# A new prologue for a fused attention and mixer kernel: first loads by heads, finer turning of the first pairs, and pair 2's norms moved into the first slot

## The chip, the cores and the metric

The kernel runs on one core of one Trainium2 chip. The metric is the device time of one execution in microseconds (us). Each kernel is executed several times, and nearly all executions of one kernel agree within 0.3%. The kernel before strays more: 6 of its 41 executions in the rounds of these runs took 388.9 to 392.6 us, the others 386.1 to 387.7. An execution more than 1.5% above the fastest of its kernel is called slow and is left out of every ratio; the quoted medians are of all executions. One execution of each kernel is recorded by the hardware profiler. Its span, from the first to the last instruction, is about 1.8 us shorter than its device time.

## The reference

The program is cosine attention with 8 batches and 12 heads, followed by a token mixer and a channel mixer.

```
q_n = q / (norm(q) + 1e-6);  k_n = k / (norm(k) + 1e-6)      # (8, 12, 448, 64)
attn = softmax(q_n @ k_n^T / 0.1) @ v
x  = attn as (8, 448, 768)
u  = x + (relu(x^T @ w_tok1) @ w_tok2)^T                     # token mixer, 448 -> 256 -> 448
out = u + relu(u @ w_ch1) @ w_ch2                            # channel mixer, 768 -> 1536 -> 768
```

## The kernel before

Two heads make a "pair"; there are 48 pairs, six to a batch. The order of instructions is written by hand, and each engine takes its own instructions in that order. A pair passes through these steps: q and k are loaded; their squares are taken on ScalarE or GpSimd; VectorE sums them; ScalarE does Ln and Exp (the square root); VectorE does the reciprocal; GpSimd or VectorE scales; TensorE transposes ("turns") and VectorE copies; TensorE scores; ScalarE takes the exp in four parts. GpSimd also issues the loads of the token weights (w1t, w2n). A "slot" is the time in which one pair's four exps run. While pair i scores, later pairs are prepared.

```
def load_rows(i, nm, src, bufs):                 # k of pairs 0 to 2 on the scalar queue, all else on sync
    ...
    (nc.scalar if nm == "k" and i < 3 else nc.sync).dma_start(...)

def norms(i, a0=0, a1=2, dve=False):
    if dve:                                      # VectorE's part
        nc.vector.tensor_reduce(out=rn, in_=ne, axis=AXX.X, op=ALU.add)
        nc.vector.reciprocal(out=rn, in_=rn)
        return
    nc.scalar.activation(out=rn, in_=..., func=AF.Ln, bias=tiny[0:n])      # ScalarE's part
    nc.scalar.activation(out=ne[:, :, 0], in_=rn, func=AF.Exp, scale=0.5)

# the prologue, from pair 0's scores on
score(0, 0)
score(0, 1)
norms(1, dve=True)
scale(1, 0)                    # GpSimd: k of pair 1
scale(1, 1, nc.vector)         # VectorE: q of pair 1
sums(2)
norms(2)
cast_v(0)
score(0, 2)
warm(8)
tpose(1)                       # eight turnings
score(0, 3)
warm(6)
norms(2, dve=True)
square(3, 1, act=True)
square(3, 0)
...
for i in range(1, NPAIR):      # slots 1 to 5
    if i == 1:
        scale(2, 0)                    # GpSimd
        scale(2, 1, nc.vector)
    else:
        scaled(i + 1)                  # both on GpSimd
        ...
    load_qk(i + 6)
    score(i, 0)
    score(i, 1)
    sums(i + 2)
    norms(i + 2)
    ...
    pv_wide(i - 1)
    norms(i + 2, dve=True)
    cast_v(i)
    square(i + 3, 0)                   # GpSimd: k of pair i + 3
    ...
    score(i, 2)
    score(i, 3)
    tpose(i + 1)
    ...
    if i == 1:
        place_w2()                     # GpSimd: copy of the second token weight
    if 2 <= i < NPAIR - 1:
        udma(i - 2)                    # u of pair 0, 1, 2 of batch 0, turned by a DMA
```

## Time and profile before

| | before |
|---|---|
| time, median of 4 executions | 386.58 us (386.31 to 392.23; without the last, a slow one, 386.36) |
| span of the profiled execution | 385.4 us |
| length of a slot | 4.19 us |
| ScalarE / GpSimd busy in 15.38 to 40.76 us | 24.51 / 24.42 of 25.38 us |
| TensorE busy after 40.76 us | 339.25 of 344.64 us |

The program has three stages. First is a chain of single waits; then six slots in which ScalarE and GpSimd are both full; then TensorE is full to the end. A delay in the first two stages moves the third. The prediction shows the lines for these. Its median of 386.36 us came from the three executions known then, the slow one among them.

### The profile page before, as it was taken

The page shows a single profiled execution, that of the slowest core. Times are in us where ns is not written, and L with a number is a line of the kernel's source. Part 1 is how long each engine was busy: PE and PEld are TensorE (multiplying, and loading weights), DVE is VectorE, ACT ScalarE, POOL GpSimd, SP SyncE. Part 2 cuts the span into 40 slices and gives each one's busy share as a digit, 9 for nine tenths or more (in the row PEclk, how much of TensorE's full clock was granted, in tenths as well). Part 3 has the DMA queues.
Part 4 walks back from the last instruction along what each step waited for, and adds up shares of the span by engine and source line. Part 5 has one row for each costly group of instructions (what it writes and reads, how often), then busy time and mean ns, then how long its engine had stood idle before and what let it go on. Part 6 is the DMA issues. An engine that isn't in the chain of part 4 may idle for free.

```text
span 385.4 us, 10226 instructions
## 1 busy us (share of the span) xinstructions
PE 372.2 (97%) x4124; PEld 243.3 (63%) x4124; DVE 217.4 (56%) x520; ACT 226.6 (59%) x398; POOL 237.8 (62%) x383
## 2 busy tenths in 40 slices
PE   5989899999999999999999999999999999999995
PEld 4566566677656666667666666667666666665564
DVE  7789766777535674557545674566544674241032
ACT  5899687845665456855675466764675466601400
POOL 8799987979567667668557767768657733000000
PEclk9799999999999999999999999999999999999998
DMA  8999999995984888768894887977996745114023
GB/s 214 263 244 235 157 235 190 226 222 112 243 191 116 200 204 201 175 168 177 213 195 117 172 204 185 197 173 181 198 217 122 134 120 133 15 54 97 0 67 99
DMA packets 115423, 64.21 MB, mean 167 GB/s; under 512 B 71728, under 2 KB 111792, under 8 KB 115376
## 3 DMA queue, kind: packets, MB, share of 16 engines
q1 hardware_dynamic: 108944, 57.62, 68.2%
q0 software_dynamic: 5616, 5.21, 8.9%
q10 hardware_dynamic: 816, 0.73, 0.7%
q8 instruction: 32, 0.52, 0.6%
q14 instruction: 15, 0.12, 0.1%
HBM read 43.45 MB, written 11.01 MB: 141 GB/s over the span
## 4 chain that ended last, share of the span: by engine, by line
PE 87%; DMA 4%; ACT 4%; DVE 2%; POOL 1%; issue 1%; ACTq 0%; DVEq 0%; POOLq 0%
PE psF L449 28%; PE psG L433 28%; PE psO L362 9%; PE psS L323 7%; PE psU L407 5%; PE psR L393 5%; DMA ut<-u 3%; ACT pt L324 3%; PE psQ L330 2%; PE psO L345 1%; DMA qf<-in_q_dram 1%; PE pst L300 1%; ACT sq L235 1%; POOL sq L237 1%; DVE ssq L253 0%
## 5 line engine op out<-in xcount | busy, mean ns | idle before, releaser
L324 ACT ACTIVATE pt<-psS 128x896 f16<-128x896 f32 (+1 forms) x156 | 132.6, 916 | 58.2 <-PE psS L323 57.8
L433 PE MATMUL psG<-ut,wc1t 128*128 128x448 f16 x576 | 116.8, 352 | 0.5 <-DMA ut<-u 0.5
L449 PE MATMUL psF<-wc2t,gt 128*128 128x384 f16 (+2 forms) x684 | 116.2, 323 | 0.0
L436 ACT ACTIVATE gt<-psG 128x448 f16<-128x448 f32 x96 | 51.8, 540 | 63.0 <-PE psG L433 63.0
L276 POOL TENSOR_TENSOR kq<-kf,rn 128x384 f16<-128x384 f32 (+1 forms) x48 | 42.8, 892 | 73.6 <-DVE rn L262 70.3
L449 PEld LDWEIGHTS <-gt 128*128 128x128 f16 x684 | 64.2, 98 | 38.0
L433 PEld LDWEIGHTS <-wc1t 128*128 128x128 f16 x576 | 53.8, 98 | 44.9 <-issue 0.7
L453 DVE TENSOR_TENSOR ost<-psF,u 128x384 f32<-128x384 f32 (+2 forms) x65 | 34.5, 531 | 57.1 <-PE psF L449 56.9
L253 DVE TENSOR_REDUCE ssq<-sq 128x15 f32<-128x960 f32 (+2 forms) x49 | 55.8, 1140 | 4.2 <-ACT sq L235 3.6
L396 DVE TENSOR_SCALAR rt<-psR 128x256 f16<-128x256 f32 x48 | 20.1, 419 | 59.5 <-PE psR L393 59.4
L276 POOL TENSOR_TENSOR kq<-qf,rn 112x512 f16<-112x512 f32 x45 | 46.9, 1043 | 3.0
L323 PE MATMUL psS<-qk 64*128 64x448 f16 x312 | 41.7, 359 | 2.7 <-DVE qk L302 2.5
L237 POOL TENSOR_TENSOR sq<-kf 128x384 f32<-128x384 f32 (+1 forms) x46 | 40.1, 872 | 1.2 <-DMA kf<-in_k_dram 1.2
L362 PE MATMUL psO<-vt,pt 128*128 128x65 f16 (+1 forms) x1056 | 40.3, 193 | 0.2 <-DVE ut L424 0.2
L237 POOL TENSOR_TENSOR sq<-qf 112x512 f32<-112x512 f32 x39 | 40.5, 1039 | 0.0
L362 PEld LDWEIGHTS <-pt 128*128 128x128 f16 (+1 forms) x1056 | 35.2, 97 | 4.0 <-PE psS L323 1.0
L366 DVE TENSOR_TENSOR x<-psO,rec 128x256 f16<-128x256 f32 x84 | 35.6, 424 | 2.9
L410 DVE TENSOR_TENSOR u<-psU,x 128x512 f16<-128x512 f32 x48 | 32.3, 674 | 4.8 <-PE psU L407 3.6
L393 PEld LDWEIGHTS <-w1t 128*128 128x128 f16 x384 | 25.0, 98 | 9.0 <-issue 2.3
L407 PEld LDWEIGHTS <-w2t 128*128 128x128 f16 x384 | 24.9, 98 | 7.8 <-issue 1.5
L393 PE MATMUL psR<-x,w1t 128*128 128x128 f16 x384 | 29.3, 219 | 0.4 <-DVE u L410 0.3
L407 PE MATMUL psU<-rt,w2t 128*128 128x128 f16 x384 | 29.3, 219 | 0.2 <-DVE qk L302 0.2
(54 smaller groups left out, 282.8 us busy)
## 6 DMA issues: line engine op xcount, KB each, us to landing
qf<-in_q_dram SPq DMA_DIRECT2D x48, 224.0 KB, 4.2
kf<-in_k_dram SPq DMA_DIRECT2D x36, 192.0 KB, 3.4
vf<-in_v_dram SPq DMA_DIRECT2D x36, 192.0 KB, 3.7
vf<-in_v_dram SPq DMA_DIRECT2D x12, 224.0 KB, 7.3
out_dram<-ost SPq DMA_DIRECT2D x8, 336.0 KB, 3.6
wc1t<-in_moe_w_ch_dram POOLq DMA_DIRECT2D x4, 576.0 KB, 10.2
wc2t<-in_moe_w_ch_dram POOLq DMA_DIRECT2D x2, 1152.0 KB, 14.0
out_dram<-ost SPq DMA_DIRECT2D x8, 288.0 KB, 3.3
```

Of the source, the lines that this page charges most:

```text
L237: nc.gpsimd.tensor_mul(out=dst, in0=src, in1=src)
L253: nc.vector.tensor_reduce(out=st["ssq"][0:n, sl], in_=st["sq"][0:n, sl], axis=AXX.X, op=ALU.add)
L276: eng.tensor_tensor(out=kq[0:p, a, 0:n].rearrange("p c g e -> p g c e"), in0=st["kq"[a]][:].rearrange("p (g c) e -> p g c e", g=2), in1=_b ...
L323: nc.tensor.matmul(psS[:, hh, 0:S], qk[hb, c * n:c * n + 128], qm[hb], start=True, stop=True)
L324: nc.scalar.activation(out=pts[i % 2][0:n, 2 * S * c:2 * S * (c + 1)].rearrange("p (h s) -> p h s", h=2), in_=psS[0:n, :, 0:S], func=AF.Ex ...
L362: nc.tensor.matmul(psO[:, m, 0:E + 1], pts[i % 2][0:n, at:at + 128], vt[0:n, i % HP, nch * hh + c, 0:E + 1], start=(old(i) and c == 0), st ...
L366: nc.vector.tensor_tensor(out=st["x"][:, :, hh * E:(hh + 1) * E], in0=psO[:, :, 0:E], in1=_bcast_free(rec[:], E), op=ALU.mult)
L393: nc.tensor.matmul(psR[:, tt], w1t[:, w1[m], tt * 128:(tt + 1) * 128], st["x"][:, m], start=(m == 0), stop=(m == 3))
L407: nc.tensor.matmul(psU[:, m], w2t[:, tt, lo:lo + 128], st["rt"][:, tt], start=(tt == 0), stop=(tt == TT - 1))
L433: nc.tensor.matmul(psG[:, 0:S], wc1t[:, dt, ct * 128:(ct + 1) * 128], ut[b][:, dt].rearrange("p m s -> p (m s)")[:, lo:lo + S], start=(dt ...
L436: nc.scalar.activation(out=gt[:, ct, (b % 2) * S:(b % 2 + 1) * S], in_=psG[:, 0:S], func=AF.Relu)
L449: nc.tensor.matmul(psF[:, 0:hi - lo], gt[:, ct, at:at + 128], wc2t[:, ct, lo:hi], start=(ct == 0), stop=(ct == CT - 1))
```

## The change

The intent is to let the first exps start sooner. Pair 0's q and k are each loaded as two halves, one head on the sync queue and one on the scalar queue, and every other load goes on sync. Pair 0's k is scaled, turned and copied in halves. Pair 1's norms come before the first exp on ScalarE, and its q and k are turned one by one, so that only four turnings stand ahead of pair 0's last score. ScalarE's load of its function table is issued earlier, too. Pair 2's norms and scalings leave the prologue for slot 1, and its q is scaled by GpSimd, not by VectorE.

```
+    def load_first(a, src):
+        t = qkv.tile([SC, QS, E], FP32, name=f"{a}f_0", tag=f"{a}f", bufs=7)
+        for g, eng in ((0, nc.sync), (1, nc.scalar)):
+            eng.dma_start(out=t[:, NCH * g:NCH * (g + 1)].rearrange("p c e -> p (c e)"),
+                          in_=src[0, g].rearrange("(p c) e -> p (c e)", c=NCH))
+        return t
 ...
-            (nc.scalar if nm == "k" and i < 3 else nc.sync).dma_start(
+            nc.sync.dma_start(
 ...
-        scale(0, 0)
+        scale_part(0, 0, 0, 2, nc.gpsimd)
+        scale_part(0, 0, 2, NCH, nc.gpsimd)
 ...                                         # sums of pair 1 split, norms(1) before the first exp
         norms(1, dve=True)
+        scale(1, 1, nc.vector)
         scale(1, 0)
-        scale(1, 1, nc.vector)
-        sums(2)
-        norms(2)
         cast_v(0)
         score(0, 2)
-        warm(8)
-        tpose(1)
+        warm(4)
+        tpose(1, 1, 2)
+        warm(4)
+        tpose(1, 0, 1)
         score(0, 3)
         warm(6)
-        norms(2, dve=True)
+        sums(2)
 ...
         for i in range(1, NPAIR):
-            if i == 1:
-                scale(2, 0)
-                scale(2, 1, nc.vector)
-            else:
+            if i > 1:
                 scaled(i + 1)
 ...
             score(i, 0)
+            if i == 1:
+                norms(2)
+                norms(2, dve=True)
+                scaled(2)
             score(i, 1)
```

More of the change, by code (lines that the diff above doesn't have):

```diff
@@ L265, in norms, with scale_part @@
         nc.scalar.activation(out=ne[:, :, 0], in_=rn, func=AF.Exp, scale=0.5)
+    def scale_part(i, a, c0, c1, eng):
+        st = pipe[i]
+        if "kq16" not in st:
+            st["kq16"] = kqs[i % 4]
+        rn = st["rn"][0:SC, lay(i)[0][a]]
+        eng.tensor_tensor(out=st["kq16"][0:SC, a, c0:c1].rearrange("p c g e -> p g c e"),
+                          in0=st["kq"[a]][:].rearrange("p (g c) e -> p g c e", g=2)[:, :, c0:c1],
+                          in1=_bcast_free(rn.rearrange("p (g c) -> p g c", g=2)[:, :, c0:c1], E), op=ALU.mult)
     def scale(i, a, eng=None):
@@ L289, in scaled, with tpose @@
         scale(i, 1)
-    def tpose(i, a0=0, a1=2):
+    def tpose(i, a0=0, a1=2, c0=0, c1=NCH):
         st = pipe[i]
@@ L296, in tpose @@
             st["qk"] = qk[:, 0:2 * NCH * n].rearrange("p (a c s) -> p a c s", a=2, c=NCH)
-        pst = ps.tile([128, a1 - a0, NCH, n], FP16, name=f"pst_{i}_{a0}", tag="b")
+        pst = ps.tile([128, a1 - a0, c1 - c0, n], FP16, name=f"pst_{i}_{a0}_{c0}", tag="b")
         for a in range(a0, a1):
-            for c in range(NCH):
-                nc.tensor.transpose(pst[:, a - a0, c, :], st["kq16"][:n, a, c].rearrange("p g e -> p (g e)"),
+            for c in range(c0, c1):
+                nc.tensor.transpose(pst[:, a - a0, c - c0, :], st["kq16"][:n, a, c].rearrange("p g e -> p (g e)"),
                                     id16[:n, :n])
-        nc.vector.tensor_copy(out=st["qk"][:, a0:a1], in_=pst[:])
+        nc.vector.tensor_copy(out=st["qk"][:, a0:a1, c0:c1], in_=pst[:])
     def tpose_dma(i):
@@ L516 @@
     with tc.manual_schedule():
-        for i in range(3):
-            load_qk(i)
+        half[0] = {}
+        pipe[0] = {"q": load_first("q", q), "k": load_first("k", k)}
+        nc.scalar.add_instruction(mybir.InstLoadActFuncSet(
+            name=nc.get_next_instruction_name(), act_func_set_id=ACT_SET_LN_EXP,
+            ins=[], outs=[]))
+        load_qk(1)
+        load_qk(2)
         load_v(0)
@@ L525 @@
         load_v(3)
-        nc.scalar.add_instruction(mybir.InstLoadActFuncSet(
-            name=nc.get_next_instruction_name(), act_func_set_id=ACT_SET_LN_EXP,
-            ins=[], outs=[]))
         weights_tok1()
@@ L535 @@
         sums(0, 0, 1)
+        norms(0, 0, 1)
         norms(0, 1, 2, dve=True)
-        norms(0, 0, 1)
         scale(0, 1, nc.vector)
         norms(0, 0, 1, dve=True)
-        scale(0, 0)
+        scale_part(0, 0, 0, 2, nc.gpsimd)
+        scale_part(0, 0, 2, NCH, nc.gpsimd)
         square(1, 1, act=True)
@@ L544 @@
         warm(40, True)
-        sums(1)
-        norms(1)
         tpose(0, 1, 2)
         warm(3, True)
-        tpose(0, 0, 1)
-        warm(5, True)
+        sums(1, 1, 2)
+        tpose(0, 0, 1, 0, 2)
+        warm(3, True)
+        sums(1, 0, 1)
         square(2, 0)
         weights_tok2()
+        norms(1)
         score(0, 0)
+        tpose(0, 0, 1, 2, NCH)
         score(0, 1)
         norms(1, dve=True)
+        scale(1, 1, nc.vector)
         scale(1, 0)
-        scale(1, 1, nc.vector)
-        sums(2)
-        norms(2)
         cast_v(0)
         score(0, 2)
-        warm(8)
-        tpose(1)
+        warm(4)
+        tpose(1, 1, 2)
+        warm(4)
+        tpose(1, 0, 1)
         score(0, 3)
         warm(6)
-        norms(2, dve=True)
+        sums(2)
         square(3, 1, act=True)
```

## The prediction

> **What bounds the kernel now.** I read the page first (busy time, slices, chain), then a table of windows for three stretches, then the timeline from 0 to 50 us with the waits. The page says that TensorE is busy nearly all the time and that the chain of work that ended last is 87% TensorE.
>
> ```profile
> PE 372.2 (97%) x4124; PEld 243.3 (63%) x4124; DVE 217.4 (56%) x520; ACT 226.6 (59%) x398; POOL 237.8 (62%) x383
> PE  5989899999999999999999999999999999999995
> ...
> PE 87%; DMA 4%; ACT 4%; DVE 2%; POOL 1%; issue 1%; ACTq 0%; DVEq 0%; POOLq 0%
> ```
>
> That is an average over stages. The change touches the start alone, so I cut the span at 15.38 us (ScalarE starts the first exp of pair 1) and at 40.76 us (first exp of pair 7). The columns are window, length, then busy us of PE, PEld, DVE, ACT, POOL, clock, DMA share, GB/s.
>
> ```profile
> 0.00:15.38 15.38, 10.53 (x96) 7.59 (x97) 11.02 (x28) 9.91 (x19) 12.83 (x32) 0.78 0.99 230
> 15.38:40.76 25.38, 22.39 (x388) 16.10 (x384) 21.91 (x47) 24.51 (x43) 24.42 (x29) 1.00 1.21 228
> 40.76:385.40 344.64, 339.25 (x3650) 219.64 (x3646) 184.47 (x446) 192.16 (x338) 200.54 (x325) 1.00 0.74 159
> ```
>
> The last stretch is TensorE's: 339.25 of 344.64 us. What happens before it only shifts it. In the middle stretch (slots 1 to 6) ScalarE is busy 24.51 of 25.38 us and GpSimd 24.42: two engines are full at once. One slot is 4.19 us (first exps at 15.38, 19.56, 23.74, 27.93). GpSimd is never idle from 18.63 us until after 45 us, so a microsecond lost there has nowhere to go. The first stretch is a chain of single waits; these timeline lines carry it.
>
> ```profile
> 7.92 1.04 POOL L276 TENSOR_TENSOR kq<-kf,rn 112x512 f16<-112x512 f32 x1 [0.49 <-DVE rn L262]
> 10.59 0.81 POOL L182 DMA_DIRECT2D w2n<-in_moe_w_tok_dram x1 [0.64 <-DMA w1t<-in_moe_w_tok_dram]
> 11.41 1.06 POOL L276 TENSOR_TENSOR kq<-kf,rn 112x512 f16<-112x512 f32 x1
> 12.53 0.93 PE L300 MATMUL pst<-id,kq 112*128 112x112 f16 x8 [0.20 <-POOL kq L276]
> 14.05 0.92 ACT L324 ACTIVATE pt<-psS 112x896 f16<-112x896 f32 x1 [0.42 <-POOL sq L237]
> 14.57 1.55 POOL L276 TENSOR_TENSOR kq<-kf,rn 112x512 f16<-112x512 f32 x1 [0.56 <-DVE rn L262]
> 18.63 0.99 POOL L185 COPY w2t<-w2n 128x896 f16<-128x896 f16 x1 [0.96 <-DMA w2n<-in_moe_w_tok_dram]
> ```
>
> The reader is to see that GpSimd's scaling of pair 1's k (11.41) stands behind the issue of the w2n load, which waits for the landing of an earlier w1t load; that TensorE's eight turnings of pair 1 (12.53) stand behind that scaling; and that pair 0's last exp (14.05) stands behind those turnings. The 0.42 there is laid to GpSimd, but TensorE's score ended at 13.94, in the same moment, and is what the exp reads.
>
> **What the Trainium skill says.** (1) "DMA: Bandwidth & Descriptors", section "Issuing engines are not separate DMA queues": transfers of the sync, scalar and gpsimd queues share the same 16 engines, and issuing from several saves only issue time. The trace agrees: pair 0's q and k, on two queues, land within half a microsecond of each other (squares at 4.36 and 4.90), and the DMA share is 1.1 from 3 us on. So splitting q over two queues brings q forward by giving it the whole rate first; it makes nothing else faster. (2) "TensorE: Matmul & The Clock Gate", section "What's actually happening": the clock halves after idle windows. The one-microsecond windows show a granted clock of 0.50 from 8 to 14 us, after TensorE stood idle 2.2 us before 7.57. (3) "SBUF — State Buffer", section "Who interferes with whom": a VectorE instruction with two SBUF inputs and a GpSimd one that reads SBUF lock each other out. The trace agrees: GpSimd's scaling took 1.55 us at 14.57, beside VectorE's scaling (14.53 to 15.22), and 1.04 us elsewhere. That each engine takes its instructions in order I read from the timeline itself: VectorE's copy of pair 0 (start 9.09) waits for nothing but the sum before it, which ends at 9.17 and overlaps it by its tail.
>
> **The change, part by part.** Start of pair 0. q arrives as two halves at the head of both queues. q's square began at 4.36 and k's at 4.90. I estimate q 0.5 us earlier (3.85), k about 0.3 earlier (4.55), as the bytes that must have landed for k are the same. The steps to pair 0's scalings (sum 0.69, Ln 0.30, Exp 0.21, sum 0.17, reciprocal 0.20, scaling 0.69) are unchanged, so they move by 0.5 us. GpSimd issues weight loads until 7.42 in both, so its two half scalings of k run about 7.43 to 8.47, against 7.92 to 8.96. Pair 1's sum, one of 1.22 us on VectorE before (7.95 to 9.17), becomes two of 0.68 with the copies of pair 0 between. Working along VectorE: copy q 7.45, sum q 7.75, copy half of k 8.4, sum k 8.5 to 9.2. Then Ln and Exp to 9.83, first exp of pair 0 at about 9.75 to 10.1, against 10.65: 0.6 to 0.9 us gained there.
>
> It does not travel. Pair 1's reciprocal ends at about 10.3 (10.38 before), and the w2n issue stands where it stood, with the w1t landing it waits for untouched. So pair 1's k scaling stays at 11.41 to 12.47. What is gained is that only four turnings (0.47 us at half clock), not eight (0.93), come before pair 0's last score: that score starts at 12.92, not 13.39, its exp at 13.58, not 14.05. ScalarE stands idle almost 1 us before it. Then square of pair 3 (0.52 until the next may start), and pair 1's first exp at **14.9 against 15.38: 0.47 us gained**.
>
> Slot 1 then pays. Pair 2's Ln and Exp, in a gap at 12.27 before, now follow that first exp: +0.53 us of ScalarE in a full slot. Their end: 14.91 + 0.80 (exp) + 0.56 = 16.27. VectorE, in order, holds pair 2's sum of norms and reciprocal (0.45 us) ahead of pair 3's sum of squares (1.22 us): reciprocal done 16.76 (14.50 before), pair 3's sum done 17.9 (16.80 before). ScalarE's Ln of pair 3 waits for that; it is free at 17.0, so **0.9 us is lost**. From there: Ln and Exp 0.47, two exps 1.6, square 0.52: pair 2's first exp at about 20.6, against 19.56.
>
> GpSimd: pair 2's k scaling starts at 16.8, not 14.57, and q's (1.03 us) is now GpSimd's too, no longer VectorE's. So 16.8 + 1.04 + 1.03 = 18.9 where it stood at 16.1; cast and square 1.57 more, the w2t copy 0.99 (its wait of 0.96 is swallowed), and pair 3's scaling begins at 21.3, **against 19.59: 1.75 us late on a full engine**. In the later slots pair i+1's copy, score and exp have about 0.4 us of slack behind GpSimd (pair 4: scaling ends 25.98, exp 27.93 after turning 0.4, copy 0.6, score 0.4). So the exps of pairs 3 to 6 come 1.75 - 0.4, about 1.4 us late, and pair 7 as well.
>
> Sum: -0.47 (fewer turnings before the last score), +0.53 (norms moved), +0.95 (Ln waits for a sum), +0.4 (GpSimd's later queue) = +1.4 us when TensorE takes over. Against that, TensorE's 0.47 us wait for a transposed u at 45.07 may vanish when TensorE comes later. Net about **+1.0 us**: 386.36 + 1.0 = 387.3 (rounded down from 387.4).
>
> **The rivals.** (a) The intent: the prologue starts 0.5 to 1 us sooner and everything follows: 385.4 to 385.9. For it: ScalarE is the full engine and starts sooner. Against it: GpSimd is as full, and it gets a scaling more and a later start. (b) The w2n issue comes free sooner, as the scalar queue's ring empties sooner and the w1t load may land earlier. Then pair 1's k scaling follows the reciprocal at 10.3, is locked out once by VectorE (1.55 us), ends 11.9, and slot 1 starts 0.98 us early; pair 2's reciprocal is at 16.2 and GpSimd still 1.2 us late: about +0.7, 387.0. (c) The last transposed u, issued at 32.01 and landing at 45.02, moves by more than the rest, as the load order changed; TensorE waits longer: up to 388.5. (d) The shift is absorbed wholly in TensorE's stretch: 386.4. Its idle after 40.76 is 5.4 us in many small pieces, so only in part.
>
> **Range and chances.** All these lie between 385.4 and 388.5; 2% is 7.7 us, more than any of them. I take 387.3 with 385.8 to 388.5: the low end keeps most of rival (a) out, whose chance I put at one in seven. Faster by 2%: 0.01; within: 0.97; slower: 0.02, for what I did not see.
>
> **What would show it.** Right: in the changed profile pair 0's first exp near 10, its last near 13.6, pair 1's first near 14.9; a wait of ScalarE for VectorE's sum of about 0.9 us near 17; GpSimd's pair 2 scaling near 16.8, pair 3's near 21; pair 2's first exp after 20; the middle stretch ending over 41.5. Wrong: w2n issued before 10.3, or GpSimd with idle time left in slots 2 to 6, or pair 2's first exp before 19.5; then the time would fall below 386.

## The result, and the profile after

The changed kernel took 388.85 us (median of 4, 388.65 to 389.07) against 386.58 us. All ratios here are made from the fast executions of the two kernels in the same rounds, so they are not quite the ratio of the quoted medians. This one is 1.0061, with a 95% interval of 1.0041 to 1.0081. By the 2% measure it is the same time, but it is 0.6% slower, and outside the range predicted.

The page of the changed kernel has hardly moved. These lines are its busy times, TensorE's slices and the chain that ended last.

```profile
PE 373.7 (96%) x4122; PEld 244.1 (63%) x4122; DVE 217.4 (56%) x522; ACT 227.1 (59%) x398; POOL 238.5 (62%) x385
...
PE   6788999999999999999999999999999999999995
...
PE 89%; ACT 4%; DVE 2%; DMA 2%; POOL 1%; issue 1%; SPq 1%; DVEq 0%; POOLq 0%
```

TensorE's first four digits are 6, 7, 8, 8 where they were 5, 9, 8, 9: fuller at the start, then emptier. The table of windows, cut at the same events as before (first exp of pair 1, first exp of pair 7), puts numbers to that. Its columns are window, length, busy us of PE, PEld, DVE, ACT and POOL, clock (the share of TensorE's full clock that was granted), DMA share and GB/s.

```profile
0.00:14.66 14.66, 10.76 (x100) 7.55 (x101) 10.47 (x28) 9.71 (x18) 12.34 (x32) 0.88 0.92 224
14.66:42.84 28.18, 23.77 (x382) 16.96 (x378) 22.36 (x49) 25.23 (x44) 26.13 (x30) 0.94 1.18 216
42.84:387.30 344.46, 339.12 (x3650) 219.57 (x3646) 184.55 (x446) 192.16 (x338) 200.06 (x324) 1.00 0.74 159
```

The first stage lost 0.72 us of its length, the slots grew by 2.80 us, and the last stage lost 0.18 us. Both full engines now have idle time in the slots: 2.95 us on ScalarE and 2.05 us on GpSimd, against 0.87 and 0.96 before.

The timeline of the first stage follows. Its columns are start, length, engine, line, operation, output and input tiles, shapes, count, and in brackets the idle time before it and what ended that.

```profile
3.58 0.63 ACT L243 ACTIVATE sq<-qf 112x512 f32<-112x512 f32 x1 [0.62 <-DMA qf<-in_q_dram]
...
7.40 1.24 POOL L280 TENSOR_TENSOR kq<-kf,rn 112x256 f16<-112x256 f32 x2
...
9.01 1.04 POOL L245 TENSOR_TENSOR sq<-kf 112x512 f32<-112x512 f32 x1 [0.37 <-DMA kf<-in_k_dram]
...
9.79 2.51 ACT L341 ACTIVATE pt<-psS 112x896 f16<-112x896 f32 x3
...
9.99 0.81 POOL L190 DMA_DIRECT2D w2n<-in_moe_w_tok_dram  x1
...
10.81 1.21 POOL L293 TENSOR_TENSOR kq<-kf,rn 112x512 f16<-112x512 f32 x1
...
12.21 0.53 PE L317 MATMUL pst<-id,kq 112*128 112x112 f16 x4
...
13.32 0.92 ACT L341 ACTIVATE pt<-psS 112x896 f16<-112x896 f32 x1 [1.02 <-PE psS L340]
...
14.66 0.91 ACT L341 ACTIVATE pt<-psS 112x896 f16<-112x896 f32 x1
```

Pair 0's q is squared at 3.58 (4.36 before) and its first exp starts at 9.79 (10.65 before). The one thing that is new is the wait at 9.01: GpSimd's square of pair 2's k now waits for that tile's load. The issue of the w2n load, pair 1's k scaling, its turning and pair 0's last exp all follow that square.

Both kernels were then profiled once more, in runs named after_again and before_again below. The start varies from execution to execution, and this second pair shows the losses with less beside them. First the changed kernel, all from its timeline.

```profile
9.69 1.04 POOL L245 TENSOR_TENSOR sq<-kf 112x512 f32<-112x512 f32 x1 [1.03 <-DMA kf<-in_k_dram]
...
11.49 1.06 POOL L293 TENSOR_TENSOR kq<-kf,rn 112x512 f16<-112x512 f32 x1
...
13.75 0.92 ACT L341 ACTIVATE pt<-psS 112x896 f16<-112x896 f32 x1 [1.38 <-PE psS L340]
...
15.08 0.91 ACT L341 ACTIVATE pt<-psS 112x896 f16<-112x896 f32 x1
...
15.88 0.31 ACT L272 ACTIVATE rn<-ssq,tiny 112x16 f32<-112x16 f32 x1
...
16.47 0.19 DVE L269 TENSOR_REDUCE rn<-ne 112x16 f32<-112x32 f32 x1 [1.76 <-ACT ne L273]
16.69 0.25 DVE L270 RECIPROCAL rn<-rn 112x16 f32<-112x16 f32 x1
16.86 1.16 DVE L261 TENSOR_REDUCE ssq<-sq 112x16 f32<-112x1024 f32 x1
...
17.02 1.04 POOL L293 TENSOR_TENSOR kq<-kf,rn 112x512 f16<-112x512 f32 x1 [2.86 <-DVE rn L270]
...
18.06 0.31 ACT L272 ACTIVATE rn<-ssq,tiny 112x16 f32<-112x16 f32 x1 [0.81 <-DVE ssq L261]
...
21.53 1.04 POOL L293 TENSOR_TENSOR kq<-kf,rn 112x512 f16<-112x512 f32 x1
...
25.97 1.22 DVE L261 TENSOR_REDUCE ssq<-sq 112x16 f32<-112x1024 f32 x1 [0.71 <-POOL sq L245]
...
27.22 0.31 ACT L272 ACTIVATE rn<-ssq,tiny 112x16 f32<-112x16 f32 x1 [0.37 <-DVE ssq L261]
```

And the kernel before, in its second profile.

```profile
9.03 1.04 POOL L237 TENSOR_TENSOR sq<-kf 112x512 f32<-112x512 f32 x1
...
15.10 1.72 ACT L324 ACTIVATE pt<-psS 112x896 f16<-112x896 f32 x2
...
16.70 0.32 ACT L264 ACTIVATE rn<-ssq,tiny 112x16 f32<-112x16 f32 x1
...
17.70 0.98 POOL L185 COPY w2t<-w2n 128x896 f16<-128x896 f16 x1 [0.29 <-DMA w2n<-in_moe_w_tok_dram]
18.63 1.04 POOL L276 TENSOR_TENSOR kq<-kf,rn 112x512 f16<-112x512 f32 x1
...
25.22 0.32 ACT L264 ACTIVATE rn<-ssq,tiny 112x16 f32<-112x16 f32 x1
```

Four things are to be seen. Pair 1's first exp starts at the same time (15.08 and 15.10), so here the prologue gained nothing. In slot 1, pair 2's Ln (15.88) and its reciprocal on VectorE (16.69) stand ahead of pair 3's sum (16.86), and ScalarE waits 0.81 us for that sum. VectorE was not busy meanwhile: it stood 1.76 us idle for pair 2's Exp (the bracket at 16.47), with pair 3's sum third in its order and that pair's last square done at 15.18. GpSimd stands idle 2.86 us for the same reciprocal, so pair 3's scaling starts at 21.53 instead of 18.63. That lateness comes back to ScalarE in slot 3: GpSimd's late square of pair 5's k holds up VectorE's sum (25.97), and ScalarE's Ln waits 0.37 us for it (27.22). The kernel before has no wait of ScalarE at either Ln.

The first exps of pairs 1, 2, 3, 4 and 7 were at 15.08, 20.83, 25.12, 29.80 and 42.64 in the changed kernel, and at 15.10, 19.43, 23.62, 27.81 and 40.65 before. Slot 1 costs 1.42 us more, slot 2 0.10, slot 3 0.49, later slots nothing. That is 1.99 us at pair 7 with the prologue's 0.02 taken off.

The spans differ by more, 387.11 - 384.74 = 2.37 us. From pair 7's first exp to VectorE's last addition the two take the same time (340.31 and 340.31 us), so 0.38 us is left for the end. This is SyncE's wait for the stores in the last 5 us of before_again; the columns are waiter, what it waited for, us in total, times, longest.

```profile
SPq L726 <- DMA out_dram<-ost: 0.9, 2, 0.7
```

The same line of the waits of after_again has one long wait and none after it.

```profile
SPq L749 <- DMA out_dram<-ost: 1.6, 1, 1.6
```

At the end, SyncE asks one after another the eight semaphores on which its DMAs land, in a fixed order and mostly 60 to 70 ns each. Successive DMAs take these semaphores in turn. Before, the last store's semaphore was next to last on the list. The change issues two DMAs more (pair 0's q and k in halves), so the last store now has the first of the eight, and seven questions remain to be asked after it has landed, where one remained before. Six more at 0.063 us make 0.38 us. From the landing of the last store to the final semaphore event took 0.93 us before and 1.31 us after.

### The profile page after: what moved, and what is told of

Its sections match the earlier page's. It is cut to its first block, busy times and chain, and to the rows that moved or that the text cites. A ratio compares the mean times of both kernels' runs of the same rounds, so it can differ in the third digit from the quotient of the medians.

```text
span 387.3 us, 10226 instructions
## 1 busy us (share of the span) xinstructions
PE 373.7 (96%) x4122; PEld 244.1 (63%) x4122; DVE 217.4 (56%) x522; ACT 227.1 (59%) x398; POOL 238.5 (62%) x385
## 4 chain that ended last, share of the span: by engine, by line
PE 89%; ACT 4%; DVE 2%; DMA 2%; POOL 1%; issue 1%; SPq 1%; DVEq 0%; POOLq 0%
PE psF L466 28%; PE psG L450 28%; PE psO L379 10%; PE psS L340 8%; PE psU L424 5%; PE psR L410 5%; ACT pt L341 3%; PE psQ L347 2%; DMA kf<-in_k_dram 2%; PE psO L362 1%; PE pst L317 1%; POOL kq L293 1%; ACT sq L243 1%; PE psO L397 0%; POOL sq L245 0%
## 5 line engine op out<-in xcount | busy, mean ns | idle before, releaser
L293 POOL TENSOR_TENSOR kq<-kf,rn 128x384 f16<-128x384 f32 (+1 forms) x47 | 41.4, 882 | 76.8 <-DVE rn L270 70.7
L293 POOL TENSOR_TENSOR kq<-qf,rn 112x512 f16<-112x512 f32 x46 | 48.0, 1043 | 3.0
```

The source lines that it names most:

```text
L293: eng.tensor_tensor(out=kq[0:p, a, 0:n].rearrange("p c g e -> p g c e"), in0=st["kq"[a]][:].rearrange("p (g c) e -> p g c e", g=2), in1=_b ...
```

## The experiments

Fifteen more runs were made, thirteen of new kernels and two repeats, all of them correct. None beat the kernel before. The table collects what their profiles show; "pair 1 to 4" is the time from pair 1's first exp to pair 4's, the cost of slots 1 to 3, and "tail" is the time from the last store's landing to the final semaphore event. In the last column is the ratio to the kernel before of the same rounds.

| kernel | pair 1's first exp | pair 1 to 4 | tail | ratio [95%] |
|---|---|---|---|---|
| before, first profile | 15.38 | 12.55 | 0.92 | |
| before_again | 15.10 | 12.71 | 0.93 | 1.0003 [0.9984, 1.0023] |
| after, first profile | 14.66 | 15.35 | 1.31 | 1.0061 [1.0041, 1.0081] |
| after_again | 15.08 | 14.72 | 1.31 | 1.0058 [1.0041, 1.0075] |
| norms2_only | 15.06 | 14.69 | 0.93 | 1.0058 [1.0039, 1.0077] |
| norms2_back | 14.95 | 12.64 | 1.30 | 1.0023 [0.9996, 1.0049] |
| warm_slot1 | 14.86 | 14.72 | 1.31 | 1.0052 [1.0031, 1.0073] |
| q2_vector | 14.67 | 14.70 | 1.30 | 1.0048 [1.0032, 1.0064] |
| w2t_vector | 14.69 | 14.17 | 1.31 | 1.0042 [1.0026, 1.0059] |
| warm_w2t_vector | 14.88 | 14.16 | 1.31 | 1.0048 [1.0028, 1.0068] |
| before_lane2 | 15.19 | 12.54 | 1.32 | 1.0001 [0.9974, 1.0028] |
| before_pe2 | 15.09 | 12.55 | 1.33 | 1.0001 [0.9974, 1.0028] |
| norms2_back_k1 | 15.56 | 13.02 | 0.86 | 1.0012 [0.9986, 1.0039] |
| norms2_back_k1_pe2 | 15.75 | 12.56 | 0.92 | 1.0022 [0.9992, 1.0051] |
| after_pe2 | 15.40 | 14.70 | 0.86 | 1.0059 [1.0047, 1.0071] |
| before_load | 14.57 | 12.75 | 1.30 | 1.0021 [1.0008, 1.0033] |
| norms2_back_pe2 | 14.86 | 12.83 | 0.86 | 1.0022 [1.0005, 1.0040] |

### Is pair 2's move the loss? norms2_back and norms2_only

norms2_back is the changed kernel with pair 2's sums, norms and scalings where they stood before.

```
         scale(1, 0)
+        sums(2)
+        norms(2)
         cast_v(0)
 ...
-        sums(2)
+        norms(2, dve=True)
 ...
+            if i == 1:
+                scale(2, 0)
+                scale(2, 1, nc.vector)
-            if i > 1:
+            else:
 ...
-            if i == 1:
-                norms(2)
-                norms(2, dve=True)
-                scaled(2)
```

> The changed kernel with pair 2's norms and scalings back where the kernel before has them (sum and Ln, Exp ahead of pair 0's third exp, q scaled by VectorE, no part of it in slot 1). If the move of these norms is the whole loss and the other parts gain: pair 1's first exp at 14.7 to 15.1, pair 3's first exp at 23.1 to 23.6 (23.74 before), time 0.3 to 0.7 us under the kernel before, 385.7 to 386.1. If the other parts of the change lose as well (loads by halves, copies in pieces): over 387.

It took 387.44 us against 386.68. norms2_only is the opposite: the kernel before, with the same lines changed the other way and nothing else.

> The kernel before with this part of the change alone: pair 2's sum behind pair 1's turnings, its Ln, Exp, reciprocal and both scalings (q's on GpSimd too) behind pair 1's first exp. If this part is the whole loss: pair 2's reciprocal after 16.3, a wait of ScalarE for VectorE's sum near 17.5, pair 3's first exp at 25.5 to 26.5, time 388.5 to 389.3. If the loss needs the other parts (order of the loads): under 387.5.

It took 389.30 us against 386.68, a ratio of 1.0058, as large as that of the full change. Its timeline has both waits of ScalarE in the same places.

```profile
18.03 0.31 ACT L264 ACTIVATE rn<-ssq,tiny 112x16 f32<-112x16 f32 x1 [0.82 <-DVE ssq L253]
...
27.18 0.31 ACT L264 ACTIVATE rn<-ssq,tiny 112x16 f32<-112x16 f32 x1 [0.37 <-DVE ssq L253]
```

So the move alone makes slots 1 to 3 about 2 us longer (14.69 against 12.71), and taking it back makes them 12.64. The profiled execution of norms2_only took 388.45 us, and the other three took 389.28 to 389.33; what made those 0.85 us longer stands in no profile. The rest of the change, on its own, does not help either: norms2_back starts pair 1's exps 0.15 us before before_again and is still 0.2% slower by its means, though its interval just reaches 1. This line of its waits shows TensorE waiting 0.7 us for a turned u.

```profile
PE psG L450 <- DMA ut<-u: 0.7, 1, 0.7
```

### Is it the clock? warm_slot1

In the first profile of the changed kernel, slot 2 lost 1.34 us (first exps of pairs 2 and 3 at 20.29 and 25.82, 5.53 us apart instead of 4.19). The table of windows shows why. The second line of it is one stretch of half clock.

```profile
16.50:19.91 3.41, 1.23 (x12) 0.63 (x13) 2.86 (x7) 2.56 (x6) 3.32 (x4) 1.00 1.13 266
19.91:23.33 3.42, 3.42 (x46) 2.68 (x44) 1.64 (x2) 2.52 (x5) 3.42 (x5) 0.50 1.12 252
```

TensorE was busy 1.23 us of 3.41 while it waited for the late scalings, and the next 3.42 us ran at half clock. The same 32 matmuls of attention times v took 1.18 us in the kernel before, as a line of its timeline shows.

```profile
19.67 1.18 PE L380 MATMUL psO<-vt,pt 112*128 112x65 f16 x32
```

In the changed kernel's timeline they took 1.97 us.

```profile
21.39 1.97 PE L397 MATMUL psO<-vt,pt 112*128 112x65 f16 x32
```

If this were the loss, keeping TensorE busy in slot 1 would return it. warm_slot1 adds idle matmuls there.

```
             score(i, 2)
+            if i == 1:
+                warm(10)
             score(i, 3)
+            if i == 1:
+                warm(12)
             tpose(i + 1)
+            if i == 1:
+                warm(10)
```

> The changed kernel with 32 more warming matmuls of the identity in slot 1 (10 before the last score of pair 1, 12 after it, 10 behind pair 2's turnings), in time in which TensorE stood idle. Clock theory (the half-rate stretch of 19.9 to 23.3 us, brought on by TensorE's idling while it waits for pair 2's late scaling, is what holds up pair 2's third exp by 1.23 us): no half clock between 18 and 24 us, pair 3's first exp at 24.5 to 24.9 instead of 25.82, time 1.0 to 1.3 us under the changed kernel, about 387.7. Queue theory (GpSimd's late queue alone holds up slots 2 and 3, the clock is harmless): pair 3's first exp within 0.2 us of 25.82, time as the changed kernel, 388.8.

The half clock was gone from slot 2, yet the kernel took 388.65 us against 386.68 (1.0052), and slots 1 to 3 took 14.72 us. That is what after_again needs without any warming: its half clock lay at 8.25 to 18.49 us, and its slot 2 ran at full clock too. (The profiled execution of warm_slot1, 389.67 us, was its longest; it met a wait for a turned u, of which more below.) norms2_only says it most plainly: its half clock ended at 14.90 us, before pair 1's first exp, so all of its slots 1 to 3 ran at full clock, and they took 14.69 us with both waits. Without the half clock, ScalarE meets its 0.37 us wait for pair 5's sum instead. The clock adds 0.6 us to one profile (15.35 against 14.72) and does not make the loss.

### Is it GpSimd's queue? q2_vector, w2t_vector and warm_w2t_vector

q2_vector gives pair 2's q scaling back to VectorE.

```
                 norms(2, dve=True)
-                scaled(2)
+                scale(2, 1, nc.vector)
+                scale(2, 0)
```

> The changed kernel with pair 2's q scaled by VectorE (0.69 us, beside GpSimd's k) and not by GpSimd (1.04 us behind it). Clock theory: pair 2's turnings end near 18.1, not 19.06, the idle time of TensorE shrinks by 0.7 to 1 us; if that is enough for the clock to stay full, pair 3's first exp comes at 24.4 to 24.8 and the time is 1.0 to 1.5 us under the changed kernel; if the half-rate stretch stays, less than 0.4 us is gained. Queue theory: GpSimd's pair 3 scaling 0.5 to 1.0 us sooner and pair 3's first exp by as much, clock or no clock.

It took 388.72 us against 386.68. GpSimd was relieved, for pair 3's scaling started at 20.60 instead of 21.53 in after_again; but VectorE, in order, now did that scaling ahead of pair 3's sum, and ScalarE's wait for the sum doubled, as its timeline shows.

```profile
18.42 0.31 ACT L272 ACTIVATE rn<-ssq,tiny 112x16 f32<-112x16 f32 x1 [1.59 <-DVE ssq L261]
```

Slots 1 to 3 took 14.70 us, as before: one wait took the place of the other. w2t_vector instead takes the copy of the second token weight off GpSimd, work for VectorE that stands ahead of nothing urgent.

```
     def place_w2():
-        nc.gpsimd.tensor_copy(out=w2t[:, :, 0:S]...
+        nc.vector.tensor_copy(out=w2t[:, :, 0:S]...
```

> The changed kernel with the 0.99 us copy that places the second token weight moved from GpSimd to VectorE (behind pair 2's copy), so that GpSimd's scaling of pair 3 starts near 20.1 instead of 21.07. Queue theory (GpSimd's late queue holds slots 2 and 3): with a full clock pair 4's first exp at 28.7 to 29.0 (30.01 in the changed kernel, 29.58 in the one with warming matmuls). Clock theory: if the half-rate stretch falls into slot 2 again, the wait of about 1.2 us for the score stays and pair 4's first exp is at 29.8 to 30.1; time as the changed kernel.

> Both: the warming matmuls in slot 1 and the copy on VectorE. If a half clock and GpSimd's queue each hide the other (either alone is replaced by the other): no wait of ScalarE over 0.2 us in slots 2 and 3, pair 4's first exp at 28.7 to 29.1, that is 0.9 to 1.3 us sooner than in the changed kernel, and time 0.5 to 1.0 us under it. If neither matters for the time: 388.5 to 388.9.

warm_w2t_vector has warm_slot1's idle matmuls besides. The two took 388.25 and 388.28 us against 386.66, where after_again in the same rounds took 388.97. In w2t_vector's timeline pair 3's scaling starts 1.34 us sooner than in after_again, and the later Ln no longer waits.

```profile
20.19 1.44 POOL L293 TENSOR_TENSOR kq<-kf,rn 112x512 f16<-112x512 f32 x1
...
26.29 0.31 ACT L272 ACTIVATE rn<-ssq,tiny 112x16 f32<-112x16 f32 x1
```

Slots 1 to 3 took 14.17 us, 0.55 us less, and the time fell by 0.7 us. So GpSimd's late queue does reach ScalarE, and about 0.6 us of the loss comes from it. The rest, the 0.53 us of pair 2's Ln and Exp and the 0.81 us wait for the sum, remains.

### How much varies by itself? after_again and before_again

These are both kernels unchanged, run to see which readings of the first profiles hold.

> The changed kernel once more, for a second profile and times on this chip. If the half-rate stretch depends on where a free-running window falls, it may lie elsewhere than at 19.9 to 23.3 us; clock theory: then pair 3's first exp is near 24.9 and the time 0.8 to 1.2 us shorter; queue theory: pair 4's first exp within 0.5 us of 30.01 and the time within 0.4 us of 388.85, wherever the stretch lies.

> The kernel before once more, for a second profile: how much of the difference is its own scatter. Expected: first exps as in the first profile within 0.3 us from pair 1 on, the third turned u landing between 43.5 and 45.5, 0.92 us from the last landing to the end, time 386.1 to 387.5.

They took 388.97 and 386.54 us. Their profiles are shown above. Three readings of the first profiles did not hold: the half clock in slot 2 of the changed kernel, the 0.47 us wait for a turned u in the kernel before (the third turned u landed at 43.24, not 45.02, and TensorE did not wait), and the prologue's gain of 0.72 us.

### What do the earlier loads do alone? before_load

before_load is the kernel before with the changed loads only (load_first, everything else on sync, the table load moved up).

> The kernel before with the loads of the change alone (pair 0 by heads over two queues, all else on the sync queue, table load early). If the loads are sound and only the tail costs: pair 0's first exp near 9.9, pair 1's first at 14.9 to 15.1, pair 4's within 0.3 us of 27.8, tail 1.31, time 0.1 to 0.4 us over the kernel before. If the loads themselves lose (later landing of the third turned u): 0.6 to 1.0 us over it, with a wait of TensorE for a turned u near 45 us.

It took 387.32 us against 386.42, a ratio of 1.0021 that excludes 1. Pair 1's first exp came 0.53 us sooner than in before_again and pair 7's 0.49 us sooner. Its half clock in the start lasted 3.42 us, not 6.83, which may be a part of that; no run parts the two. Nothing of the gain arrived. TensorE came to the turned u of pair 2 before it had landed (issued at 31.40, landed at 44.80), as this line of its waits shows.

```profile
PE psG L440 <- DMA ut<-u: 0.8, 1, 0.8
```

From its first channel matmul to its seventh it took 2.94 us where before_again took 1.93, so 1.01 us was lost there, and the tail grew by 0.37 us. -0.49 + 1.01 + 0.37 = 0.89 us; the spans differ by 385.57 - 384.74 = 0.83 us and the medians by 0.90 us. In this profile the earlier start in the slots was worth nothing, as this transfer landed no sooner. Asked for between 31.40 and 32.01 us in before, before_again, before_lane2 and before_load, it landed between 43.24 and 45.02.

### Is the wait for the turned u worth taking away? before_pe2, norms2_back_pe2, norms2_back_k1_pe2, after_pe2

In these four the third u is turned by TensorE and not by a DMA, in four bases: before, norms2_back, norms2_back_k1 (below) and after.

```
-            if 2 <= i < NPAIR - 1:
+            if 2 <= i < NPAIR - 2:
                 udma(i - 2)
 ...
             if i == NPAIR + 1:
+                upose(i - 5)
                 tok2(i - 2, pe=True)
```

> The kernel before with that last part alone: pair 2's u turned by TensorE. Wait theory: the 0.47 us wait at 45.07 is gone, 0.2 us of turning is added, time 0.2 to 0.4 us under the kernel before. Otherwise: the same or up to 0.2 slower.

> All that the runs spoke for: pair 2's norms back in the prologue, pair 0 by heads and k in halves kept, pair 2's u turned by TensorE, which also sets the tail right. Pair 4's first exp at 27.5 to 27.8, no wait for a turned u, tail 0.86; time 0.1 to 0.5 us under the kernel before, 386.2. If that is lost in the scatter: within 0.3 of the kernel before.

> The same, and pair 2's u turned by TensorE in slot 7 beside pairs 3 to 5, not by the DMA. Wait theory (the third turned u lands at 44.2 to 47 us, hardly moved by when it is issued, and TensorE's first channel matmuls wait for it, 0.7 us in the kernel with norms back; so any gain of the prologue ends there): no wait for a turned u near 45 us, the first 6 channel matmuls without a gap, and the prologue's gain of 0.35 us comes through: time 0.3 to 0.8 us under the kernel before, near 386.0. If the wait is only a symptom of TensorE being early: no gain, 387.0.

> The changed kernel with pair 2's u turned by TensorE, so one transfer less: the last store's semaphore is the last in SyncE's list, not the second. Tail theory: 0.85 us from the last landing to the end (1.31 in the changed kernel), the slots as they were (pair 4's first exp at 29.6 to 30.0), time 0.3 to 0.6 us under the changed kernel, near 388.5. If the tail does not reach the measured time: 388.8 to 389.1.

They took 387.15 (against 386.96), 387.07 (386.42), 387.86 (386.96) and 388.78 us (386.42). None of the four profiles has a wait for a turned u (after and norms2_back_k1 had none to lose), but no ratio moved by more than the intervals allow: norms2_back and norms2_back_pe2 are at 1.0023 and 1.0022, after and after_pe2 at 1.0061 and 1.0059. The turnings on TensorE cost 0.30 us of their own (from pair 7's first exp to the first channel matmul 3.60 us in after_pe2, 3.30 in after_again), and leaving one DMA out moves the semaphore of the last store again, so the tail changes too. For after_pe2 the sum is +0.30 - 0.45 us, which the timing cannot tell from nothing. In norms2_back_pe2 a good part of the loss lies outside the span: by the medians of the fast executions of these rounds its time is 0.67 us over that of the kernel before (387.07 and 386.40), its span only 0.3 (384.9 and 384.6). Why is open. As a mend it failed.

### Is the tail real? before_lane2 and norms2_back_k1

before_lane2 is the kernel before with the v loads of pairs 0 and 1 in two halves each, two DMAs more and nothing else. norms2_back_k1 is norms2_back with pair 0's k in one load again, one DMA more than before.

```
+            if nm == "v" and i < 2:                     # before_lane2
+                for g in range(2):
+                    nc.sync.dma_start(out=t[:, NCH * g:NCH * (g + 1)]..., in_=src[h0 + g]...)
+                return t
```

```
-        pipe[0] = {"q": load_first("q", q), "k": load_first("k", k)}    # norms2_back_k1
+        pipe[0] = {"q": load_first("q", q)}
+        pipe[0]["k"] = qkv.tile([SC, QS, E], FP32, ...)
+        nc.scalar.dma_start(out=pipe[0]["k"]..., in_=k[0, 0:2]...)
```

> The kernel before with two loads more: v of pairs 0 and 1 in two halves each, so that all later transfers sit two places further in the ring of eight transfer semaphores, as in the changed kernel. Tail theory (at the end SyncE asks the semaphores one after the other, some 65 ns each; the last store's semaphore is then second in that list, not next to last, so that seven or eight questions follow its landing): 1.3 us from the last store's landing to the end of the span, against 0.92 before; time 0.3 to 0.5 us over the kernel before. If the tail is chance: 0.9 to 1.0 us, and no difference in time beyond 0.2.

> The changed kernel with pair 2's norms back in the prologue and pair 0's k in one load on the scalar queue (one load less than the halves, so that the last store's semaphore is the last in SyncE's list). Tail theory: about 0.85 us from the last landing to the end; time 0.3 to 0.5 us under the same kernel with k in halves, 387.0, if pair 0's last exp comes within 0.2 us of 13.64. If the tail is chance: 387.3 to 387.5.

The profiles agree with the count but for one. With as many DMAs as before the tail is 0.92 or 0.93 us (four profiles), with one more 0.86 (three), with two more 1.30 to 1.32 (nine), with one less 1.33 (before_pe2). That last one does not follow from the count: two questions remain there after the last store's, which makes about 1.0 us. The question just before the last store's, on a semaphore that had landed at 383.35, ended 0.41 us after its predecessor, at 383.97, when the last store had landed at 383.68. Such late answers come in other profiles too (382.33 to 382.74 in before_again), but there before the last landing, where they cost nothing. In the times the tail cannot be seen: before_lane2 took 387.24 us against 386.96, a ratio of 1.0001 with an interval of 0.27% on either side, and 0.38 us is 0.1%. Two of the ten fast executions of the kernel before in those rounds took 388.89 and 389.12 us, though. Without them its mean is 386.82 us, and before_lane2's 387.26 is 0.44 over it; but they were picked out afterwards, so this proves nothing. So the tail is shown in the spans, but not by timing. norms2_back_k1 got the short tail and took 387.66 us against 386.96, while its pair 1 started at 15.56, later than in any other kernel but its own variant; its time says nothing of the tail alone.

## Why the prediction was wrong

The direction and the place of the loss were right; the size was not: +1.0 us predicted, +2.3 us measured by the medians. Here are the steps against after_again and before_again, whose spans differ by 2.37 us.

| step of the prediction | predicted | measured |
|---|---|---|
| fewer turnings before the last score | -0.47 | -0.02 here; -0.27 on the mean of the profiles |
| pair 2's norms in slot 1 | +0.53 | +0.53 |
| ScalarE's Ln waits for pair 3's sum | +0.95 | +0.81 |
| GpSimd's later queue | +0.4 | +0.59 in slots 2 and 3 |
| TensorE's wait for a turned u vanishes | about -0.4 | 0.00 |
| the end of the program | not looked at | +0.38 |

**Right.** Slot 1 pays, and by the two mechanisms named: pair 2's Ln and Exp in a full slot, and VectorE's reciprocal of pair 2 ahead of pair 3's sum. In the first profile GpSimd's pair 2 scaling started at 16.59 (predicted 16.8) and pair 3's at 21.07 (21.3), and pair 2's first exp at 20.29 (20.6); in after_again these stood at 17.02, 21.53 and 20.83, so the agreement is within the scatter. The three slot terms sum to 1.88 us and measured 1.99 - (-0.02) = 2.01 us, of which 0.08 us in slot 1 is not assigned. norms2_only shows that the move of pair 2 is the cause, w2t_vector what GpSimd's queue has in it, and norms2_only and warm_slot1 that it is not the clock. That the 0.81 us come from VectorE's order is read from the timeline and fits q2_vector, where one instruction more ahead of the sum made it 1.59 us; no run put pair 2's reciprocal behind that sum.

**Right in size by luck: GpSimd's +0.4.** The prediction led GpSimd's lateness to the exps by scaling, turning, copy and score, with 0.4 us of slack there (its own lines give 0.55: 27.93 - 25.98 less 0.4, 0.6 and 0.4). In after_again most of it came another way, by GpSimd's late square of pair 5's k, VectorE's sum and ScalarE's Ln (0.37 us, in slot 3). The sum that led to 21.3 for pair 3's scaling gives 21.46 as written.

**The failed step: "TensorE's 0.47 us wait for a transposed u at 45.07 may vanish when TensorE comes later".** There was a wait of that size in the one profile of before at hand, and in the first pair of profiles it did vanish. But before_again and before_lane2, which are the same in that place, have none: there was nothing to win back. The profiled execution took 387.20 us, and the prediction set the wait off against a median of 386.36 us of other executions. It took one execution's wait for a property of the kernel. That took 0.4 us off the sum and brought 1.4 down to 1.0; measured between after_again and before_again it is 0.00.

**Not foreseen: the end.** The prediction said that what happens before TensorE's stage only shifts it. The two extra DMAs cost 0.38 us at the very end, by way of the order of semaphores.

**Mis-sized: the prologue's -0.47.** Its mechanism is right (pair 0's last score does come behind four turnings), but pair 1's k scaling was thought pinned at 11.41 by w2n's issue, "with the w1t landing it waits for untouched". That pin, too, was one execution's: in before_again w2n's issue (10.01) waits for no landing and the scaling starts at 10.83. In the changed kernel stands a new wait. Pair 2's k was sent from the scalar queue to the end of the sync queue, and in ten of the twelve profiles with that load, GpSimd waits 0.37 to 1.36 us for it. (The other two are norms2_back_k1 and its variant, where pair 0's k comes later and GpSimd is busy longer.) In the five with the load on the scalar queue it does not wait. w2n's issue and pair 1's k scaling follow at once, so this scaling starts anywhere from 10.81 (after) over 11.49 (after_again) to 11.80 (after_pe2), and pair 1's first exp follows 3.59 to 3.85 us behind it: 14.66, 15.08, 15.40. Over the nine profiles whose loads and whose pairs 0 and 1 are those of the changed kernel the mean of that exp is 14.89, over five with the old prologue 15.16: 0.27 us gained, not 0.47. On these means the scaling itself starts 0.11 us later (11.14 and 11.03) and the way from it to the exp is 0.38 us shorter. That the k2 load's place is the cause of the wait is what the brackets of the timeline say; no run put only that load back on the scalar queue.

**The rivals.** (a), that everything follows the earlier start, is refuted: before_load starts earlier and ends later. (b), an earlier w2n, came in the first profile (9.99, scaling at 10.81), by which the prediction would have been wrong the other way, with the time under 386; pair 1's first exp came 0.72 us sooner there, and the time was 389.07. (c), a longer wait for the turned u, was not in the changed kernel's own profiles; it came in warm_slot1 (landing at 47.02, 0.8 us) and, in another shape, wherever TensorE was handed over to early (before_load, norms2_back). (d), absorption, is refuted.

The parts do not add up simply: the move of pair 2 costs 2.2 us alone (norms2_only by its ratio) and the rest 0.9 us alone (norms2_back by its ratio), more than the 2.3 us of both together. norms2_back meets a wait of 0.7 us for the turned u which the changed kernel, coming later, does not, and 2.2 + 0.9 - 0.7 = 2.4. But the intervals of these ratios are some 0.7 to 1 us on either side, so that the sum is not shown.

**What stays open.** Why the third turned u lands where it does: it was issued between 31.40 and 34.09 us in the profiles, and landed between 43.24 and 47.02 with little relation to that. Whether the 0.38 us at the end is exactly the time it costs, which timing cannot resolve. And why time and span differ by 1.9 to 2.2 us in five kernels and by about 1.8 us in the others.

## What to carry to other kernels

Before work is moved out of a prologue into a steady stage, look at which engines are full there, and at what stands behind the moved work in each engine's order: two small instructions of VectorE (0.19 and 0.25 us) cost ScalarE 0.81 us, because they had to wait for ScalarE's own Exp, and a sum that ScalarE needed next stood behind them. A wait read from one profile is that execution's; profile the unchanged kernel twice before a gain is booked on it, and give a tile that moves to another queue's end a look at who waits for it. When a change of some tenths of a microsecond alters the number of DMAs, read the last few microseconds too.

## What the Trainium skill lacked or had wrong

- "TensorE: Matmul & The Clock Gate", section "What's actually happening": its 3.4 us free-running window agrees (half-rate stretches of 3.41, 6.83 and 10.24 us in the starts of the profiles, begun anywhere from 7.77 to 10.34 us). But it speaks of an idle window, without a measure: here a window with TensorE busy 1.23 of 3.41 us was followed by 3.42 us at half clock, and one with 2.01 us busy (q2_vector, 6.93 to 10.34) by 6.83 us. The busy share alone does not tell: in the same profile a window with 1.87 us busy (17.17 to 20.58) was followed by full clock.
- No page that I read tells how a program's own wait for its last stores goes: SyncE asks eight DMA semaphores in a fixed order, mostly at 60 to 70 ns each, so the number of DMAs moves the time from the last landing to the end, 0.86 to 1.32 us in 16 profiles; the 17th, 1.33 us, does not follow the count.
- "DMA: Bandwidth & Descriptors", section "DMA Transpose (X-bar)": I found no figure there for how long a transposed tile takes behind queued loads. Here the first two took 5.8 to 8.5 us from issue to landing, and the third, where a DMA turned it, 10.7 to 13.4 us.
